# One order of all work replaced by another in a block-sparse attention kernel with a SoLU layer behind it

## The chip, the cores and the metric

The kernel runs on one core of a Trainium2 chip. The metric is device time in microseconds, the median of several executions; less is better. A core has five engines that run side by side, each through its own list of instructions in order: TensorE (PE: matrix multiplies, and transposes done as multiplies), VectorE (DVE), ScalarE (ACT), GpSimd (POOL) and SyncE (SP), which here only issues transfers. They wait for one another through semaphores. Transfers between the device memory and the core's memory (SBUF) are moved by 16 DMA engines.

## The reference

```python
# attention: batch 4, 8 heads, 768 positions, 64 wide; blocks of 32 positions
scores = scale * np.matmul(q, k.transpose(0, 1, 3, 2))
mask = np.abs(blk_i - blk_j) <= window          # neighbouring blocks
mask = mask | (blk_i == 0) | (blk_j == 0) | (blk_i == n_blocks - 1) | (blk_j == n_blocks - 1)
...                                             # and three sampled blocks for each block of queries
attn = softmax(np.where(mask, scores, -1000000000.0))
x = (attn @ v)                                  # brought to 3072 rows of 512
# the layer behind it: 512 -> 1024 -> 512
h = x @ w_in
solu = h * softmax(h)
ln = (solu - mu) / np.sqrt(var + 1e-06) * g_ln
out = ln @ w_out
```

## The kernel before

Nothing in the program is sorted out by a scheduler at run time. The kernel makes a list of some 1,130 operations (`op(...)`), each with the engine that runs it, the operations it depends on, the buffers it takes and the buffers whose last reader it is. A list of numbers, `ORDER` (lines 16 to 68), says in which order they are emitted. `Plan.run` walks through that list, checks that what an operation depends on came before it, and hands out buffers in the order in which they come free:

```python
        order = [self.ops[k] for k in ORDER]
        for o in order:
            assert all(d.done for d in o.deps + o.after)
            for p in o.take:
                o.slots[p] = self.pools[p].pop(0)
            for a, names in o.last_of:
                ...
                        self.pools[p].append(a.slots[p])
```

So `ORDER` sets two things: the order of the instructions on every engine, and which buffer each of them uses. An instruction whose input or buffer is late holds up everything behind it on its engine.

The operations, with the names used below (b is the batch, t one of three tiles of 256 queries, pr one of four pairs of heads, j one of 24 tiles of 128 output rows):

- Loads on SP (line 332): `load6/k1.0` brings the keys of batch 1, pair 0; there are three staging buffers each for k, q and v. Batch 0 is loaded in parts (`load2`, `load4`). The second weight matrix (`w_out`, line 377, two parts of 1 MB), the vector g (line 371) go through SP too; the first weight matrix (`w_in`, line 366) goes through POOL.
- Casts to bf16 on POOL: `cast6/q2.1` and so on (line 495 for k and q of batches 1 to 3, line 418 for v, lines 426 and 484 for batch 0). A cast gives the staging buffer free.
- Turning k and q so that the 64 columns of a head lie along the partitions: for batch 0 on TensorE with a copy by VectorE (`turn4`, `turn8`, lines 439 and 426); for batches 1 to 3 by a transposing transfer on SP (`cross_kq/k1.3`, line 497) and two copies by VectorE (`split/k1.3.0` and `.1`, line 501). A split overwrites the keys or queries of four pairs earlier, and waits for the last score that uses them. The mask of blocks is made at the start by POOL and VectorE, spread out by two small multiplies (`maskmm2`, `maskmm4`, line 305), and carried as 24 extra rows of k and q.
- Attention: for each (b, t, pr) three `score`s of 128x1024 on TensorE (line 523) into one of two score buffers, three exponentials on ScalarE (`exp`, line 528), one `pv` of 24 multiplies (line 542) into one of two accumulator banks (`mbank`), then `recip` and `norm` on VectorE (lines 551 and 554), which write x and give the bank free. There are eight buffers for the results of `exp`, and a `pv` frees three of them.
- The layer: x of 256 rows is turned by a transfer on SP (`cross_x`, line 585; on TensorE for the first and last tile, `turn2`, line 575). For each j two `feed4` (line 602) into one buffer of two banks, `silu_e` on ScalarE (line 624), `mult` on VectorE (line 627, which makes u and gives that buffer free), `stats` and `aggr` on VectorE (lines 634 and 637), `z2`, `vr` and `rs` on POOL (lines 640, 643 and 676). u is turned by a transfer on SP (`cross_u`, line 707). Two `out4` on TensorE (line 717) into an `mbank`, `scale` on VectorE (line 723, gives the bank free), `store` on SP (line 726). The last two tiles, 22 and 23, are done in halves (`half_e`, `half_m`, `half_s`, `feed3` and `feed1`, `outh`, `scaleh`).
- The weights `w_out` are multiplied with g and centred on VectorE (`wsum`, line 391; `wo`, line 405) between 20 and 54 us.
- `spare512`, `spare256`, `spare128`: multiplies of constants on TensorE that nobody reads (line 774), of 512, 256 or 128 columns. `SPARES` (line 15) lists their widths; they too have places in `ORDER`.

Of the kernel before, what the change touches and what calls it, by code (L numbers as in the profile page):

```python
# [11 lines left out]
ACT = mybir.ActivationFunctionType  # L12
PSUM = bass.MemoryType.PSUM

SPARES = (512, 512, 512, 512, 512, 512, 256, 256, 256, 256, 128, 128, 128, 128, 128, 128)
ORDER = [
# [52 lines left out]
]  # L69


# [15 lines left out]
class Plan:  # L87
# [9 lines left out]
    def op(self, name, eng, emit, deps=(), take=None, last_of=(), after=()):  # L97
        o = Op(name, eng, emit, deps, after, take, last_of)
        self.ops.append(o)
        return o  # L100
# [23 lines left out]
def kernel(  # L124
# [647 lines left out]

    for w in SPARES:
        s = op(f"spare{w}", "PE", lambda o, w=w: nc.tensor.matmul(
# [40 lines left out]
```

## Time and profile before

| | |
|---|---|
| time, median of 3 runs | 210.71 us (210.54 to 211.74) |
| profiled execution, its own time | 211.4 us |
| its span, first to last instruction | 209.7 us |
| granted TensorE clock in the record | 1.00 |
| busy: PE, DVE, ACT, POOL | 198.8, 147.6, 169.9, 72.1 us |
| instructions | 5757 |
| moved by DMA | 41.29 MB |

The profile shows one execution. A timeline row gives the start of an instruction or of a row of like ones, the time that it was busy, the engine, the line of the source, the operation, what it writes and reads, and in brackets how long the engine was idle before it and who ended that. "SPq" is SP's queue of transfer issues, where a row's time is the time to issue and not to land. Multiplies on TensorE overlap, so that the busy time of a row of them is longer than the distance to the next row; the distance between starts is what counts. An engine off the path that sets the end may be idle without cost.

### The profile page before, as it was taken

To read this page: it belongs to the slowest core of one execution; us is meant where nothing else is said; L and a number is where in the kernel's file an instruction comes from. 1 tells how busy PE (TensorE), PEld (TensorE's weight loads), DVE (VectorE), ACT (ScalarE), POOL (GpSimd) and SP (SyncE) were. 2 spreads that over 40 slices of the span, in tenths; PEclk is the share of its full clock that TensorE was granted. 3 is DMA by queue.
4 is the path that set the end of the run, shared out by engine and by line. 5 is a ranking of instruction groups with operands and counts; after the bars stand their busy time and mean duration, and the time that the engine had idled before them with its cause. 6 is when DMAs were issued, how large, how long until landed. Compare 5 with 4: busy or idle time off the path is not lost.

```text
span 209.7 us, 5757 instructions
## 1 busy us (share of the span) xinstructions
PE 198.8 (95%) x2257; PEld 140.0 (67%) x2289; DVE 147.6 (70%) x327; ACT 169.9 (81%) x210; POOL 72.1 (34%) x153
## 2 busy tenths in 40 slices
PE   7899999999979999989999999999999999999993
PEld 4698787666656676756656676766667677767452
DVE  5576579999997575896588626687876536449863
ACT  3399999997759879878788779998789989988470
POOL 7685322526057116424430811612120310010272
PEclk9999999999999999999999999999999999999999
DMA  5999998999999999989999997787842372542313
GB/s 137 301 360 343 322 164 296 181 315 301 222 316 265 307 188 260 280 181 282 194 323 204 234 196 175 99 174 95 188 100 53 92 111 69 87 100 53 101 62 143
DMA packets 71088, 41.29 MB, mean 197 GB/s; under 512 B 52236, under 2 KB 67092, under 8 KB 71060
## 3 DMA queue, kind: packets, MB, share of 16 engines
q1 hardware_dynamic: 69968, 39.86, 83.3%
q0 software_dynamic: 1056, 1.05, 3.0%
q8 instruction: 18, 0.29, 0.6%
q14 instruction: 10, 0.08, 0.1%
q10 hardware_dynamic: 36, 0.00, 0.0%
HBM read 23.07 MB, written 6.29 MB: 140 GB/s over the span
## 4 chain that ended last, share of the span: by engine, by line
PE 70%; DMA 8%; DVE 7%; ACT 5%; issue 4%; POOL 2%; SPq 2%; POOLq 0%; ACTq 0%
PE spairs L523 23%; PE mbank L717 15%; PE hpair L602 14%; PE mbank L542 13%; DMA uT<-u 5%; ACT ex L528 4%; PE hfirst L439 2%; DVE w_out_sb L405 2%; DMA qst<-in_q_dram 2%; PE sones L602 2%; DVE qT L501 2%; DMA kst<-in_k_dram 1%; DVE u L627 1%; SPq L332 1%; DVE kT L501 1%
## 5 line engine op out<-in xcount | busy, mean ns | idle before, releaser
L528 ACT ACTIVATE ex<-spairs 128x1024 bf16<-128x1024 f32 x144 | 140.6, 1025 | 25.4 <-PE spairs L523 24.1
L523 PE MATMUL spairs<-qT,kT 88*128 88x256 bf16 x576 | 82.3, 272 | 0.8 <-ACT ex L528 0.5
L523 PEld LDWEIGHTS <-kT 88*128 88x128 bf16 x576 | 53.1, 97 | 21.9 <-issue 3.0
L717 PE MATMUL mbank<-w_out_sb,uT 128*128 128x512 bf16 x172 | 45.5, 379 | 1.3 <-DMA uT<-u 0.3
L542 PEld LDWEIGHTS <-ex 128*128 128x128 bf16 x1152 | 41.5, 97 | 7.7 <-issue 3.0
L542 PE MATMUL mbank<-va,ex 128*128 128x65 bf16 x1152 | 42.9, 193 | 1.6 <-DVE x L554 0.8
L602 PE MATMUL hpair<-w_in_sb,xT 128*128 128x512 bf16 x156 | 42.8, 379 | 1.6 <-DMA xT<-x 0.4
L627 DVE TENSOR_TENSOR u<-hpair,e 128x1024 bf16<-128x1024 f32 x22 | 26.8, 1218 | 12.1 <-ACT e L624 11.8
L634 DVE BATCH_NORM_STATS2 bs<-u 128x6 f32<-128x512 bf16 x44 | 29.4, 680 | 0.3
L602 PEld LDWEIGHTS <-xT 128*128 128x128 bf16 x192 | 18.0, 97 | 14.8 <-DMA xT<-x 1.6
L717 PEld LDWEIGHTS <-uT 128*128 128x128 bf16 x184 | 17.0, 97 | 14.1 <-DMA uT<-u 1.3
L723 DVE TENSOR_SCALAR ot<-mbank,rs 128x512 f32<-128x512 f32 x23 | 17.2, 747 | 12.5 <-PE mbank L717 5.6
L643 POOL TENSOR_SCALAR vr<-z,mv 128x1 f32<-128x1 f32 x22 | 6.1, 276 | 55.0 <-DVE mv L637 52.4
L624 ACT ACTIVATE e<-hpair 128x1024 bf16<-128x1024 f32 x22 | 22.5, 1023 | 2.3 <-POOL vr L643 0.9
L551 DVE RECIPROCAL r<-mbank 128x4 f32<-128x4 f32 x48 | 8.3, 174 | 16.9 <-PE mbank L542 16.6
L554 DVE TENSOR_TENSOR x<-mbank,r 128x256 bf16<-128x256 f32 x48 | 19.6, 412 | 0.5
L495 POOL CAST qb<-qst 128x768 bf16<-128x768 f32 x12 | 10.7, 895 | 15.5 <-DMA qst<-in_q_dram 15.5
L418 POOL CAST va<-vst 128x768 bf16<-128x768 f32 x16 | 13.6, 853 | 6.7 <-DMA vst<-in_v_dram 6.6
L640 POOL TENSOR_TENSOR z<-z 128x1 f32<-128x1 f32 x22 | 4.2, 195 | 31.9 <-ACT e L624 30.6
L676 POOL TENSOR_TENSOR rs<-vr,neg_half 128x1 f32<-128x1 f32 x24 | 13.9, 581 | 1.2
L501 DVE COPY qT<-qx 64x768 bf16<-64x768 bf16 x24 | 11.8, 490 | 2.8 <-DMA qx<-qb 2.1
L495 POOL CAST kb<-kst 128x768 bf16<-128x768 f32 x12 | 10.1, 845 | 9.8 <-DMA kx<-kb 7.5
(90 smaller groups left out, 120.6 us busy)
## 6 DMA issues: line engine op xcount, KB each, us to landing
vst<-in_v_dram SPq DMA_DIRECT2D x16, 384.0 KB, 5.0
out_dram<-ot SPq DMA_DIRECT2D x23, 256.0 KB, 3.0
kst<-in_k_dram SPq DMA_DIRECT2D x15, 384.0 KB, 5.4
qst<-in_q_dram SPq DMA_DIRECT2D x12, 384.0 KB, 5.2
w_out_f<-in_moe_w_out_dram SPq DMA_DIRECT2D x2, 1024.0 KB
qst<-in_q_dram SPq DMA_DIRECT2D x4, 256.0 KB, 7.4
w_in_sb<-in_moe_w_in_dram POOLq DMA_DIRECT2D x2, 512.0 KB, 9.6
q0st<-in_q_dram SPq DMA_DIRECT2D x4, 128.0 KB, 2.9
```

What stands on the lines that cost most here:

```text
L495: ca = op(f"cast6/{nm}{b}.{pr}", "POOL", lambda o: nc.gpsimd.tensor_copy(out=cb[o.slot], in_=st[ld.slot].rearrange("p h c d -> p c h d")), ...
L501: got.append(op(f"split/{nm}{b}.{pr}.{hh}", "DVE", lambda o, hh=hh: nc.vector.tensor_copy(out=dst[0:D, sl, :, hh, :], in_=cx[t.slot][hh * ...
L523: nc.tensor.matmul(s[:, m, :], kT[0:KR, sl, jc, hh, :], qT[0:KR, sl, 2 * t : 2 * t + 2, hh, :], start=(m % 2 == 0), stop=(m % 2 == 1))
L528: exs.append(op(f"exp/{b}.{t}.{pr}.{n}", "ACT", lambda o, so=so: nc.scalar.activation(out=exb[o.slot], in_=banks("s", "pairs")[so.slot], f ...
L542: nc.tensor.matmul(acc(o)[:, qt, hh, :], exb[exs[n].slot][:, m, qt * P : (qt + 1) * P], va[i][:, 2 * pr + hh, jc, :], start=first, stop=(n ...
L554: nrm = op(f"norm/{b}.{t}.{pr}", "DVE", lambda o: nc.vector.tensor_tensor(out=xb[x_of[b, t].slot][:, :, 2 * pr * D : (2 * pr + 2) * D].rea ...
L602: nc.tensor.matmul(hb(n) if last else hb()[:, n, :], xTb[xt[0].slot][:, qt, c, :], w_in_sb[n][:, c, :], start=(c == 0), stop=(c == KD - 1))
L624: zs = op(f"silu_e/{j}", "ACT", lambda o: nc.scalar.activation(out=eb[o.slots["e"]], in_=hb().rearrange("p a f -> p (a f)"), func=ACT.Exp, ...
L627: us = op(f"mult/{j}", "DVE", lambda o: nc.vector.tensor_mul(out=ub[o.slot], in0=hb().rearrange("p a f -> p (a f)"), in1=eb[zs.slots["e"]] ...
L634: bs.append(op(f"stats/{j}.{n}", "DVE", lambda o, n=n: nc.vector.bn_stats(out=bsb[(bs[0] if bs else o).slot][:, n, :], in_=ub[us.slot][:, ...
L717: nc.tensor.matmul(mbank[m0.slot], uTb[ut[0].slot][:, KF // 2 * n + f, :], w_out_sb[n][:, f, :], start=(n == 0 and f == 0), stop=(n == 1 a ...
L723: fo = op(f"scale/{j}", "DVE", lambda o: nc.vector.tensor_scalar(out=otb[o.slot], in0=mbank[os_[0].slot], scalar1=rsb[rs.slot], scalar2=No ...
```

## The change

`ORDER` is another list, and `SPARES` has 19 entries for 16: 4,096 columns in all for 4,864. Everything else is the same text; the operations and their dependencies are the same.

```diff
-SPARES = (512, 512, 512, 512, 512, 512, 256, 256, 256, 256, 128, 128, 128, 128, 128, 128)
+SPARES = (512, 512, 512, 256, 256, 256, 256, 128, 128, 128, 128, 128, 128, 128, 128, 128, 128, 128, 128)
 ORDER = [
-    0, 9, 21, 31, 1115, 3, 7, 1126, 32, 1123, 1121, 1114, 4, 33, 22, 13, 1119, 12, 2, 14, 1116, 24, 35, 11, 15,
...
+    1124, 0, 21, 31, 1115, 2, 115, 11, 32, 1114, 3, 4, 5, 13, 33, 12, 14, 22, 15, 86, 9, 6, 16, 35, 23, 17, 18,
...
```

Written out by name, engine by engine, the two orders run close together. These are the places that the prediction speaks of. The start, on each engine:

```
PE   before  11 spares (3,584 columns) turn4/k0.0 maskmm2 spare512 spare256 turn4/q0.0 turn8/k0.2 spare256 score/0.0.0.0
             turn4/q1.0 score/0.0.0.1 turn4/k1.0 turn8/k1.2 score/0.0.0.2
     after   spare128 spare512 spare512 maskmm2 turn4/k0.0 spare256 spare128 spare512 spare128 turn4/q0.0 turn8/k0.2 spare128
             turn4/q1.0 score/0.0.0.0 score/0.0.0.1 spare128 turn8/k1.2 turn4/k1.0 score/0.0.0.2
POOL before  ... ident sel2 sel2 cast4/k0.0.2 cast2/q0.1.0 maskc2 cast6/k0.1.0 sel4 cast6/k0.2.0
     after   ... ident maskc2 ones cast4/k0.0.2 sel4 cast2/q0.1.0 sel4 cast6/k0.1.0 vones cast6/k0.2.0
SP   before  k0.0 q0.0 k0.0 q0.1 k0.1 k0.2 q0.2 q0.3 v0.0 k0.3 q0.0 q0.1 g v0.1 v0.2 w_out q0.2 v0.3 k1.0 q0.3 w_out
     after   k0.0 q0.0 k0.0 g q0.1 k0.1 k0.2 k0.3 v0.0 q0.2 q0.3 v0.1 q0.0 w_out q0.1 q0.2 v0.2 v0.3 k1.0 q0.3 w_out
```

From 45 to 65 us:

```
POOL before  z2/1 q1.2 k1.3 vr/0 v1.0 q1.3 rs/0 q2.1 v1.2 v1.1 vr/1 rs/1 q2.0          (k, q, v: casts)
     after   z2/2 k1.3 q1.3 vr/0 z2/1 v1.1 rs/0 v1.2 vr/1 rs/1 v1.3 q2.0 k2.0 vr/2 rs/2 v2.0 k2.2 z2/3 vr/3 v2.1 rs/3 q2.1
SP   before  ... cross_kq/q1.2 cross_kq/q1.3 v1.2 cross_kq/k1.3 q2.1 cross_x/0.2 k2.1 store/0 q2.2 q2.3 cross_u/2 v1.3
     after   ... cross_kq/k1.2 cross_u/2 cross_kq/q1.3 cross_kq/k1.3 k2.0 cross_x/0.2 v1.2 store/0 q2.1 v1.3 q2.2 v2.0 store/1 cross_u/3
PE   before  pv/1.0.0 out4/1.0 score/1.0.2.0 out4/1.1 score/1.0.2.1 score/1.0.2.2 feed4/4.0 pv/1.0.1 score/1.0.3.0 score/1.0.3.1
             feed4/4.1 score/1.0.3.2 pv/1.0.2 out4/2.0
     after   pv/1.0.0 score/1.0.2.0 score/1.0.2.1 pv/1.0.1 out4/1.0 score/1.0.2.2 score/1.0.3.0 out4/1.1 feed4/4.0 score/1.0.3.1
             feed4/4.1 score/1.0.3.2 pv/1.0.2 score/1.1.0.0 out4/2.0
DVE  before  split/q1.3.1 stats/1.0 mult/3 norm/1.0.0 split/k1.3.0 split/q1.3.0 split/k1.3.1
     after   norm/1.0.0 split/k1.3.1 split/q1.3.1 recip/1.0.1 split/q1.3.0 split/k1.3.0 mult/3 stats/1.0
```

From 85 to 92 us, and the end:

```
DVE  before  recip/1.2.0 stats/7.0 split/q2.1.1 split/k2.0.1 norm/1.2.0 scale/5
     after   split/q2.1.0 recip/1.2.0 aggr/6 split/q2.1.1 mult/7 scale/5 norm/1.2.0
PE   before  pv/1.2.0 out4/5.0 score/1.2.1.2 score/1.2.2.0 out4/5.1 score/1.2.2.1 pv/1.2.1
     after   pv/1.2.0 score/1.2.1.2 out4/5.0 score/1.2.2.0 out4/5.1 score/1.2.2.1 feed4/8.0 score/1.2.2.2 pv/1.2.1
DVE  before  half_m/22.0 aggr/21 half_m/22.1 half_m/23.0 uevac4/22.0 scale/20 half_m/23.1 scale/21 uevac4/23.0
     after   half_m/22.0 scale/19 half_m/23.0 half_m/22.1 uevac4/22.0 aggr/21 half_m/23.1 scale/20 uevac4/23.0 scale/21
```

102 rows, old and new, of the table ORDER are left out of this document.

## The prediction

> **What bounds the kernel now.** I read the page's busy times first, then the stages, then the chain that ended last, and last the queues at the places where that chain leaves TensorE. The page's first row and a table of stages (columns: stage, its length, busy us and instruction count of TensorE, its weight loads, VectorE, ScalarE and POOL, then granted clock, DMA share and GB/s):
>
> ```profile
> PE 198.8 (95%) x2257; PEld 140.0 (67%) x2289; DVE 147.6 (70%) x327; ACT 169.9 (81%) x210; POOL 72.1 (34%) x153
> 0.00:10.00 10.00, 7.95 (x59) 5.32 (x60) 5.10 (x18) 4.03 (x5) 6.52 (x21) 1.00 0.73 213
> ...
> 36.00:57.00 21.00, 19.74 (x211) 13.44 (x212) 20.27 (x41) 17.83 (x25) 7.68 (x11) 1.00 1.15 256
> 57.00:68.00 11.00, 9.43 (x99) 6.30 (x99) 9.45 (x18) 8.24 (x10) 6.93 (x12) 1.00 1.24 296
> ...
> 88.00:110.00 22.00, 21.06 (x226) 14.00 (x227) 16.59 (x36) 17.32 (x21) 9.50 (x16) 1.00 1.16 242
> 110.00:206.60 96.60, 95.35 (x1030) 64.94 (x1044) 63.26 (x144) 80.20 (x106) 23.39 (x59) 1.00 0.62 123
> ```
>
> From 110 us to the last matmul TensorE is idle for 96.60 - 95.35 = 1.25 us: nothing but fewer columns would shorten that part, and the orders hold the same columns there. An order can win in front of it: 2.05 us idle in the first 10, 1.26 in 36 to 57 (where VectorE, 20.27 of 21.00, is the bound), 1.57 in 57 to 68, 0.94 in 88 to 110. The chain of waits shows what the third of these is:
>
> ```profile
> 54.20 3.81 DMA qst<-in_q_dram
> ...
> 58.06 0.83 POOL qb L495
> ...
> 58.91 0.37 SPq L332
> ...
> 59.33 5.53 DMA uT<-u
> ...
> 64.90 0.39 PE mbank L717
> ...
> 65.94 0.88 PE spairs L523 x8
> 66.81 0.87 PE mbank L717 x4
> 67.68 0.47 PE spairs L523 x4
> 68.14 0.73 PE mbank L542 x24
> ```
>
> Read from the bottom: out4/2.0 waits for the transposed u of row tile 2, whose transfer was issued at 59.33, because SP stood behind a load of q (58.91) that wanted a buffer, which POOL gave free with a cast (58.06) that waited for another load (54.20). The last four rows give what dense work costs: two scores 0.88, half an output or feed 0.87, one score 0.45, one pv 0.73. Against these, TensorE's own timeline (start, busy, idle before and who ended it):
>
> ```profile
> 57.50 1.07 PE L523 MATMUL spairs<-qT,kT 88*128 88x256 bf16 x8
> 58.99 1.04 PE L602 MATMUL hpair<-w_in_sb,xT 128*128 128x512 bf16 x3 [0.43 <-DMA xT<-x]
> 60.74 0.89 PE L542 MATMUL mbank<-va,ex 128*128 128x65 bf16 x24 [0.71 <-POOL va L418]
> ...
> 63.67 0.90 PE L542 MATMUL mbank<-va,ex 128*128 128x65 bf16 x24
> 64.90 1.04 PE L717 MATMUL mbank<-w_out_sb,uT 128*128 128x512 bf16 x3 [0.33 <-DMA uT<-u]
> ```
>
> Scores at 57.50 need 0.88, feed4/4.0 starts at 58.99: 0.61 lost to the transposed x. That feed needs 0.87, pv/1.0.1 starts at 60.74: 0.88 lost to the cast of v. pv/1.0.2 needs 0.73, the output starts at 64.90: 0.50 lost. Together 2.0 us, more than the idle column says, since a matmul's modelled end hides 0.2 to 0.3 of each gap.
>
> **The change, part by part.** Instructions on VectorE, ScalarE, POOL and SP are the same ones in another order. TensorE has 19 filler matmuls of 4,096 columns for 16 of 4,864.
>
> *POOL and SP at 50 to 65 us.* The rows of POOL, then SP, then VectorE:
>
> ```profile
> 58.06 0.82 POOL L495 CAST qb<-qst 128x768 bf16<-128x768 f32 x1 [7.32 <-DMA qst<-in_q_dram]
> 58.83 1.86 POOL L418 CAST va<-vst 128x768 bf16<-128x768 f32 x2
> ...
> 54.89 1.24 SPq L585 DMA_TRANSPOSE xT<-x  x1
> ...
> 46.66 1.21 DVE L627 TENSOR_TENSOR u<-hpair,e 128x1024 bf16<-128x1024 f32 x1
> ...
> 53.38 0.42 DVE L554 TENSOR_TENSOR x<-mbank,r 128x256 bf16<-128x256 f32 x1
> ```
>
> POOL stood 7.32 us in cast6/q2.1, with the casts of v1.2 and v1.1 behind it; u of tile 2 was ready at 46.66 + 1.21 = 47.9 and its transfer left at 59.33. After the change cast6/v1.1 stands directly behind vr/0, cast6/q2.1 stands fifteen instructions behind it, and cross_u/2 stands on SP ahead of cross_kq/q1.3, far in front of those loads of q: it leaves at about 49. So the waits of 0.88 and 0.50 have lost what made them. The 0.61 stays: cross_x/0.2 needs norm/0.2.3, which ran at 53.38 and has 0.35 us (one split) more VectorE work ahead of it, and this stage is VectorE's. With the 0.6 of the opening (below) the transfer leaves at 54.9 to 55.2 and feed4/4.0 can start at about 59.2, against 58.99. But TensorE has by then also done pv/1.0.1 and one score more, 0.73 + 0.45 = 1.18 us of work that it had ahead of it before. Sum up to pv/1.0.3: -1.18 - 0.88 - 0.50 + 0.2 = -2.36; I keep +0.3 for short waits of VectorE for the splits of k1.3, which now stand ahead of mult/3, and take -2.1. That includes the opening. Bounds: +0.5 (all three waits return elsewhere and the opening is paid) and -2.9 (opening free).
>
> *88 to 110 us.* VectorE's rows and TensorE's pv/1.2.1:
>
> ```profile
> 88.69 0.95 DVE L501 COPY qT<-qx 64x768 bf16<-64x768 bf16 x1 [0.37 <-PE spairs L523]
> 89.56 0.97 DVE L501 COPY kT<-kx 64x768 bf16<-64x768 bf16 x1
> 90.56 0.42 DVE L554 TENSOR_TENSOR x<-mbank,r 128x256 bf16<-128x256 f32 x1
> ...
> 89.82 0.60 PE L523 MATMUL spairs<-qT,kT 88*128 88x256 bf16 x4
> 91.04 0.89 PE L542 MATMUL mbank<-va,ex 128*128 128x65 bf16 x24 [0.62 <-DVE x L554]
> ```
>
> There are two accumulator banks; pv/1.2.1 waits for norm/1.2.0 to empty one, and that stood behind two splits. The score at 89.82 needs 0.45, so 91.04 - 90.27 = 0.77 us are lost. In the new order the splits of q2.1, mult/7 and scale/5 stand before norm/1.2.0, about 3.1 us after score/1.2.1.2, but TensorE has out4/5.0, a score, out4/5.1, a score, feed4/8.0 and a score before pv/1.2.1: 3 x 0.87 + 3 x 0.45 = 3.96 us. The bank is free in time. The stage's other idle time is 0.94 - 0.62 = 0.32; I take -0.8 for the stage, between 0 (other splits take their place) and -1.1.
>
> *The opening.* TensorE, then ScalarE, POOL, SP:
>
> ```profile
> 0.83 3.15 PE L774 MATMUL mbank<-const-bfloat16-1.0 128*128 128x512 bf16 x11 [0.83 <-PEq L799]
> 3.77 0.63 PE L439 MATMUL hfirst<-ident,kc 128*88 128x128 bf16 x4
> 4.63 0.20 PE L305 MATMUL mbank<-allow_b,selp 24*128 24x24 bf16 x2 [0.23 <-DVE allow_b L287]
> ...
> 9.03 0.87 PE L439 MATMUL hfirst<-ident,kc 128*88 128x128 bf16 x12 [0.99 <-POOL kc L426]
> ...
> 10.37 13.76 ACT L528 ACTIVATE ex<-spairs 128x1024 bf16<-128x1024 f32 x14 [1.19 <-PE spairs L523]
> ...
> 8.14 0.83 POOL L426 CAST kc<-kst 128x768 bf16<-128x768 f32 x1 [2.02 <-DMA kst<-in_k_dram]
> ...
> 8.40 0.41 SPq L371 DMA_DIRECT2D g_row<-in_moe_g_ln_dram  x1
> ```
>
> From 10.37 on ScalarE runs its exponentials end to end; what starts that run is the third one, and it hangs on the load of k0.1, cast at 8.14. Now three fillers of 1,152 columns stand ahead of the mask's matmul and then TensorE waits for allow_b; the table of g is issued ahead of k0.1 on SP, 0.41 us and its gap; POOL waits for the mask (copy to qc, memset of onesf) before it casts the rest of k0.0, and turn4/q1.0 stands ahead of the first score, so the first exponential is about a microsecond later. That is before the point that counts: k0.1's cast moves from 8.14 to at most 8.6. Besides, the eleven fillers took 2.94 us for 3,584 columns, 0.82 ns a column, and the twelve transposes at 9.03 took 0.70 for 1,536, 0.46 ns: TensorE starts at about half pace, though the granted clock reads 1.00 in the stage's row. With its dense work beginning near 4.5 instead of 0.83 the slow pace should last longer. Between that cast and the third exponential lie twelve transposes and a score, 12 x 128 + 4 x 256 = 2,560 columns, 2,560 x 0.36 ns = 0.92 us more if all are slow; I count half of that, and 0.1 to 0.2 for the load: +0.6 for the start of the run; bounds 0.1 (only the load) and 2.5 (slow for four more exponentials). The load of w_out is moved ahead of q of pairs 1 and 2 and v0.2, v0.3; by the bytes ahead of them these land at 18 to 23 us, each just ahead of its use, so I cost that at nothing; a late v0.2 would hold back the exponentials one for one.
>
> [...]
>
> *The end.* half_m/23.1 stands ahead of scale/20 now, but TensorE works up to 206.6 either way: -0.1. For 110 us on, where the margins are other ones, I add +0.3 (0 to +1.0).
>
> Sum against the profiled execution's own 211.4 (span 209.7 and 1.7 around it): -2.1 - 0.8 - 0.1 + 0.3 = -2.7, so 208.7. That execution is 0.7 over the median of 210.71; in terms of the median, **208.0**.
>
> **The rivals.** [...]
> (B) The waits only change place: TensorE, held up by VectorE's splits of k1.3 or by its wo products, has not done the 1.18 us before feed4/4.0, and the late 0.8 returns: 208.0 + 1.2 + 0.8 = 210.0. For it: VectorE is full from 36 to 57.
> (C) Slower: the load of v1.2, before at 51.38, now stands on SP behind cross_x/0.2 and leaves at about 56.1. This row is the loads of v:
>
> ```profile
> DMA to landing us min/median/max: 3.7/5.0/9.5
> ```
>
> With 5.0 its cast ends at 61.95, just as TensorE asks for pv/1.0.2; behind it on POOL stand vr/1, rs/1 and the cast of v1.3, behind those scale/1 and store/1. With 9.5 it ends at 66.45 against pv/1.0.2 at 63.67 before: 2.8 later, less the 0.50, less the late 0.8 or not: 210.7 + 2.8 - 0.5 + 0.3 - 0.1 = 213.2, or 212.4 with the late gain; I take 213.0, since v1.3 follows on the same queue. It decides against the change from a landing of 7.7 on.
>
> **How the numbers follow.** Forecast 0.52, A 0.14, B 0.18, C 0.16. One per cent (about what a measurement of this kernel can tell from no change) is 208.6 and 212.8. The forecast's own range is 206.4 to 209.2; 0.46 of its 0.52 lie below 208.6, 0.06 above. A and B lie within. C lies above, and I count into its 0.16 the like of it at other loads. Faster 0.46, same 0.06 + 0.14 + 0.18 = 0.38, slower 0.16. The range runs from all gains at their bounds (-2.9 - 1.1 - 0.1 = -4.1, with a little kept back: 206.2) to just short of C: 212.6.
>
> **What would show it.** Right: POOL's idle time of 7 us before a cast of q is gone, cross_u/2 leaves SP near 49, TensorE reaches pv/1.0.3 near 66 instead of 67.98, no idle time over 0.4 at 88 to 110, and the end of the last matmul some 2.7 earlier. The opening: third exponential at 10.5 to 11.2. Wrong: a wait of TensorE for v over 0.5 us near 62, slow matmuls after 10 us, or a TensorE idle time of over 2 us after 110.

## The result, and the profile after

The changed kernel takes 207.97 us, the median of 6 executions (207.44 to 208.95), against 211.23 (210.34 to 212.09, 6) for the kernel before: a ratio of 0.990, 95% interval 0.9864 to 0.9936. In a later set of runs it came to 207.59 (207.04 to 208.71, 12), ratio 0.9899 (0.9865 to 0.9932). Medians in this document are over all executions; the ratios and their intervals leave out executions more than 1.5% above the fastest of the same kernel in the same set, and so a ratio is not always the quotient of two medians.

The profiled execution of the changed kernel took 207.91 with a span of 206.2 (before 211.4 and 209.7). Its busy times and the same table of stages as in the prediction (TensorE, its weight loads, VectorE, ScalarE, POOL, granted clock, DMA share, GB/s):

```profile
PE 198.3 (96%) x2292; PEld 141.3 (69%) x2292; DVE 146.8 (71%) x327; ACT 170.5 (83%) x210; POOL 73.0 (35%) x153
0.00:10.00 10.00, 6.65 (x49) 5.02 (x50) 4.98 (x16) 3.28 (x5) 7.34 (x24) 1.00 0.71 214
...
36.00:57.00 21.00, 20.52 (x246) 14.59 (x244) 19.96 (x42) 19.32 (x25) 8.46 (x12) 1.00 1.13 215
57.00:68.00 11.00, 11.00 (x131) 7.62 (x128) 9.72 (x21) 9.38 (x12) 4.01 (x6) 1.00 1.02 299
68.00:88.00 20.00, 20.00 (x227) 13.85 (x226) 14.37 (x32) 17.28 (x22) 10.82 (x22) 1.00 1.14 244
88.00:110.00 22.00, 22.00 (x257) 15.22 (x256) 16.11 (x36) 18.98 (x23) 6.34 (x12) 1.00 1.21 269
110.00:203.10 93.10, 92.70 (x1008) 62.96 (x1006) 62.53 (x141) 78.07 (x102) 24.11 (x59) 1.00 0.60 131
```

TensorE's idle time, stage by stage: 3.35 us in the first ten (before 2.05), 0.48 for 1.26 from 36 to 57, 0.00 for 1.57 from 57 to 68, 0.00 for 0.94 from 88 to 110, and 0.40 for 1.25 behind 110. The opening is dearer than before, every stage from 36 us on is cheaper, and from 57 to 110 us TensorE never stops. The place where the chain of waits stood before, on TensorE, POOL, SP and VectorE:

```profile
58.45 1.04 PE L523 MATMUL spairs<-qT,kT 88*128 88x256 bf16 x8
59.32 1.03 PE L717 MATMUL mbank<-w_out_sb,uT 128*128 128x512 bf16 x4
60.19 1.03 PE L602 MATMUL hpair<-w_in_sb,xT 128*128 128x512 bf16 x4
...
66.57 0.89 PE L542 MATMUL mbank<-va,ex 128*128 128x65 bf16 x24
...
60.94 0.82 POOL L418 CAST va<-vst 128x768 bf16<-128x768 f32 x1 [6.31 <-DMA vst<-in_v_dram]
...
49.39 1.26 SPq L707 DMA_TRANSPOSE uT<-u  x1
...
55.17 1.23 SPq L585 DMA_TRANSPOSE xT<-x  x1
56.45 0.77 SPq L332 DMA_DIRECT2D vst<-in_v_dram  x1
...
52.01 1.40 DVE L405 SCALAR_TENSOR_TENSOR w_out_sb<-w_out_f,g_sb,wbar 128x512 bf16<-128x512 f32 x2
```

No row of TensorE there has a bracket: nothing is waited for. POOL still stands 6.31 us, but in a cast that is early enough. pv/1.0.3 starts at 66.57 instead of 67.98.

To add up waits that the modelled ends hide, I take the distance between the starts of successive operations on TensorE, less what each takes in dense work (0.45 for a score, 0.73 for a pv, 0.87 for half a feed or output, 0.22 to 0.45 for turns, 0.053 for 128 columns of filler, my estimate, where the traces of before and of the changed kernel show 0.054 to 0.060 at the fast pace), and call it the loss. The slow pace of the opening counts as loss too. The table gives it up to and with the operation named, then from there on; a small negative number is the rounding of those durations, and differences of 0.3 or less can be such rounding. "New" and "old" say which order a kernel (below) has in that stretch.

| kernel | to score/0.2.0.2 (34 us) | to pv/1.0.3 (67) | to score/2.0.2.2 (107) | to the end |
|---|---|---|---|---|
| before | old 5.91 | old 3.99 | old 1.32 | old 0.33 |
| changed | new 7.61 | new 1.20 | new -0.27 | new -0.45 |
| changed, again | new 7.35 | new 0.93 | new -0.26 | new -0.49 |
| h1, first run | old 6.66 | new 0.96 | new 0.76 | new -0.48 |
| h1, second run | old 6.37 | new 0.65 | new 0.77 | new -0.39 |
| h2 | new 8.39 | old 3.47 | old 0.69 | old 0.06 |
| c1 | old 5.85 | old 4.61 | new 0.41 | new -0.58 |
| c2 | old 5.82 | old 3.41 | old 1.03 | new -0.52 |
| b1, b2, b3 | 6.15, 5.37, 6.56 | 2.52, 4.41, 2.69 | 1.84, 0.43, 1.28 | -0.06, -0.05, -0.30 |

### The profile page after: what moved, and what is told of

Same layout as the page of the kernel before. It is cut to its first block, busy times and chain, and to the rows that moved or that the text cites. A ratio compares the mean times of both kernels' runs of the same rounds, so it can differ in the third digit from the quotient of the medians.

```text
span 206.2 us, 5792 instructions
## 1 busy us (share of the span) xinstructions
PE 198.3 (96%) x2292; PEld 141.3 (69%) x2292; DVE 146.8 (71%) x327; ACT 170.5 (83%) x210; POOL 73.0 (35%) x153
## 4 chain that ended last, share of the span: by engine, by line
PE 67%; DMA 15%; POOL 7%; issue 4%; DVE 4%; SPq 1%; ACT 0%; POOLq 0%; DVEq 0%; ACTq 0%
PE spairs L523 22%; PE mbank L717 16%; PE hpair L602 15%; PE mbank L542 12%; DMA qst<-in_q_dram 5%; DMA kst<-in_k_dram 4%; DMA vst<-in_v_dram 3%; DMA kx<-kb 3%; POOL kb L495 1%; PE sones L602 1%; SPq L497 1%; POOL va L418 1%; DVE u L654 1%; POOL rs L676 1%; DVE ot L723 1%
## 5 line engine op out<-in xcount | busy, mean ns | idle before, releaser
L523 PE MATMUL spairs<-qT,kT 88*128 88x256 bf16 x576 | 84.4, 274 | 0.9 <-ACT ex L528 0.6
L717 PE MATMUL mbank<-w_out_sb,uT 128*128 128x512 bf16 x184 | 47.1, 379 | 0.0
L602 PE MATMUL hpair<-w_in_sb,xT 128*128 128x512 bf16 x176 | 45.0, 379 | 0.0
L723 DVE TENSOR_SCALAR ot<-mbank,rs 128x512 f32<-128x512 f32 x23 | 17.2, 747 | 11.2 <-POOL rs L676 6.9
L418 POOL CAST va<-vst 128x768 bf16<-128x768 f32 x16 | 14.6, 910 | 14.1 <-DMA vst<-in_v_dram 13.9
L495 POOL CAST qb<-qst 128x768 bf16<-128x768 f32 x12 | 10.2, 856 | 7.5 <-DMA qst<-in_q_dram 6.0
L501 DVE COPY kT<-kx 64x768 bf16<-64x768 bf16 x24 | 9.2, 383 | 2.2 <-DMA kx<-kb 1.8
```

Source lines behind the costliest of these rows:

```text
L418: ready_v[(b, pr)] = op(f"cast6/v{b}.{pr}", "POOL", lambda o: nc.gpsimd.tensor_copy(out=va[i][:, 2 * pr : 2 * pr + 2, :, 0:D], in_=vst[ld. ...
L495: ca = op(f"cast6/{nm}{b}.{pr}", "POOL", lambda o: nc.gpsimd.tensor_copy(out=cb[o.slot], in_=st[ld.slot].rearrange("p h c d -> p c h d")), ...
L523: nc.tensor.matmul(s[:, m, :], kT[0:KR, sl, jc, hh, :], qT[0:KR, sl, 2 * t : 2 * t + 2, hh, :], start=(m % 2 == 0), stop=(m % 2 == 1))
L602: nc.tensor.matmul(hb(n) if last else hb()[:, n, :], xTb[xt[0].slot][:, qt, c, :], w_in_sb[n][:, c, :], start=(c == 0), stop=(c == KD - 1))
L717: nc.tensor.matmul(mbank[m0.slot], uTb[ut[0].slot][:, KF // 2 * n + f, :], w_out_sb[n][:, f, :], start=(n == 0 and f == 0), stop=(n == 1 a ...
L723: fo = op(f"scale/{j}", "DVE", lambda o: nc.vector.tensor_scalar(out=otb[o.slot], in0=mbank[os_[0].slot], scalar1=rsb[rs.slot], scalar2=No ...
```

## The experiments

**The start and the rest apart.** h1 has the order of before up to score/0.1.0.2 (which TensorE starts at 21 to 23 us) and the changed order behind it; h2 the other way round. The fillers go with the parts: h1 has 5,632 columns of them and h2 3,328. Before, on the same chip: 211.10 (209.15 to 212.07).

```diff
-ORDER = the changed order
+ORDER = h1: before up to score/0.1.0.2, then what is left, in the changed order
+ORDER = h2: changed order up to score/0.1.0.2, then what is left, in the order of before
```

> The old order up to score/0.1.0.2 (about 21 us), the new order behind it. Theory (the two stretches are worth what they are worth by themselves: the new start costs 1.4 us, all later changes give 4.7): about 206.5, 1.4 under the new order; the exponentials run from 10.4 and silu_e/0 starts near 35.0. Rival (the two halves of an order only fit together): new waits at the seam, 208 or more.

> The new order up to score/0.1.0.2, the old one behind it. Theory: the start alone costs 1.4 us, so about 212.6 against 211.2 for the old order. Rival (the gain is spread over the whole order, the start costs nothing at the end): 211 or less.

Measured: h1 206.54 (205.97 to 208.37), ratio 0.9807 (0.973 to 0.9884); h2 211.55 (210.44 to 211.90), ratio 1.0021 (0.9949 to 1.0092). The gain comes with the new rest and not with the new start. What the new start costs with the old rest behind it, h2 can't tell: its interval runs from 1.1 us below before to 1.9 above, and the expected 1.4 lies in it, as does nothing at all. Its trace loses 8.39 up to 34 us.

**What the new start costs.** ScalarE's exponentials in the changed kernel, and the first exponential of the layer (`silu_e/0`, line 624) as the mark; the last row is the same mark before:

```profile
8.81 6.00 ACT L528 ACTIVATE ex<-spairs 128x1024 bf16<-128x1024 f32 x6 [4.22 <-PE spairs L523]
15.07 2.85 ACT L528 ACTIVATE ex<-spairs 128x1024 bf16<-128x1024 f32 x3 [0.25 <-PE spairs L523]
...
18.52 1.94 ACT L528 ACTIVATE ex<-spairs 128x1024 bf16<-128x1024 f32 x2 [0.60 <-PE spairs L523]
20.35 0.19 ACT L256 ACTIVATE warm<-const-float32-0.0 1x1 f32<-1x1 f32 x1
...
36.39 1.03 ACT L624 ACTIVATE e<-hpair 128x1024 bf16<-128x1024 f32 x1
...
35.02 1.04 ACT L624 ACTIVATE e<-hpair 128x1024 bf16<-128x1024 f32 x1
```

The third exponential starts at 8.81 + 2 x 1.00 = 10.81, 0.44 later than before's 10.37; two gaps of 0.25 and 0.60 follow, and 0.09 for the small activation that the new order puts between exponentials: 1.38 in all, and the mark is 1.37 later. The cast of k0.1, which the prediction had at up to 8.6, began at 8.09 (before 8.14), so the 0.44 is not the load's. Three kernels try to take parts of the loss away. In a1 the loads of q0.2 and q0.3 come first again:

```diff
 SP    (loads)
-k0.2 k0.3 v0.0 q0.2 q0.3 v0.1
+k0.2 q0.2 k0.3 q0.3 v0.0 v0.1
 POOL  (casts)
-cast6/v0.1 ... cast2/q0.3.0
+cast2/q0.3.0 cast6/v0.1
```

> The new order, but on SP the loads of q0.2 and q0.3 go ahead of k0.3 and v0.0 as in the old one, and on POOL the cast of q0.3 goes ahead of the cast of v0.1. Theory (most of what the start lost went at the sixth to tenth exponential, where the queries of pairs 2 and 3 were late: gaps of 0.25 and 0.60): about 0.85 faster than the new order, 207.1, both gaps gone, third exponential still near 10.8. Rival (slow pace of TensorE made the loss): no change, 208.0.

Measured: 208.34 (207.47 to 209.01), ratio 0.9875 (0.9803 to 0.9947). The loads alone are not it: the gaps stay, at 0.34 and 0.60.

```profile
15.28 2.85 ACT L528 ACTIVATE ex<-spairs 128x1024 bf16<-128x1024 f32 x3 [0.34 <-PE spairs L523]
18.73 1.94 ACT L528 ACTIVATE ex<-spairs 128x1024 bf16<-128x1024 f32 x2 [0.60 <-PE spairs L523]
```

They end with scores, and what stands ahead of those scores on TensorE is its own order of turns: turn4/q2.0 behind score/0.0.1.2, and turn4/q3.0, turng, turn8/q0.2, a filler and turn2 between score/0.0.2.2 and score/0.0.3.0. In a2 the early fillers are back, 2,432 columns ahead of the mask's multiply, to have TensorE at its fast pace earlier:

```diff
 PE
-spare128 spare512 spare512 maskmm2
+spare128 spare512 spare512 spare512 spare512 spare512 spare512 spare256 spare128 maskmm2
```

> The new order with 2,432 more columns of fillers ahead of the mask's first multiply, 3,584 as in the old one. Rival of a1 (slow pace): the fast pace comes near 6 us instead of near 9.4, the third exponential moves from 10.8 to about 10.4, and 0.4 us or more of the loss goes: 207.5. Theory of a1 (loads): the gaps of 0.25 and 0.60 stay; if only the load of k0.1 gates the third exponential, no change at all.

Measured: 208.06 (207.98 to 208.29), ratio 0.9866 (0.98 to 0.9932), no different from the changed kernel's 0.990. Its first scores and exponentials:

```profile
7.22 1.04 PE L523 MATMUL spairs<-qT,kT 88*128 88x256 bf16 x8
...
7.86 5.82 ACT L528 ACTIVATE ex<-spairs 128x1024 bf16<-128x1024 f32 x6 [3.74 <-PE spairs L523]
14.82 2.86 ACT L528 ACTIVATE ex<-spairs 128x1024 bf16<-128x1024 f32 x3 [1.13 <-PE spairs L523]
...
12.22 0.40 POOL L426 CAST qc<-q0st 128x256 bf16<-128x256 f32 x1 [2.92 <-DMA q0st<-in_q_dram]
```

The scores are fast and the exponentials begin 0.95 earlier, and then wait 1.13 instead of 0.25 for the seventh score. In front of that score on TensorE stand turn4/q2.0 and pv/0.0.0. The last row is the cast that the first of them waited for, and the cast of v for the second stands behind it: with the slow pace gone, the load of q0.2 came too late. a1 has that load early (its cast began at 9.58) and keeps the slow pace; no kernel here has both, so that the two together cost nothing is not shown. a3 is a1 with the turns moved ahead of the scores, and VectorE's copies with them:

```diff
 PE    (beside the edit of a1)
-score/0.0.1.2 ... turn4/q2.0     turn8/k3.2 ... turn4/k3.0     score/0.0.2.2 ... turn4/q3.0
+turn4/q2.0 score/0.0.1.2         turn4/k3.0 turn8/k3.2         turn4/q3.0 score/0.0.2.2
```

> The new order with the loads and casts of a1 and, on TensorE, turn4/q2.0 ahead of score/0.0.1.2, turn4/k3.0 ahead of turn8/k3.2 and turn4/q3.0 ahead of score/0.0.2.2 (with VectorE's copies), as in the old order. Theory (the gaps of 0.25 and 0.60 come from turns that stand between a score and the next, with no buffer free to work ahead): both gaps of ScalarE go, 0.8 us faster than the new order, about 207.2. Rival (other work then fills the same time, or the data are late there anyway): gaps move on, 208.

Measured: 208.35 (207.32 to 209.05), 0.9948 (0.9924 to 0.9972) of before on its chip (median there 209.77), so it is no faster than the changed kernel was against before. The 0.60 is gone, and its place is taken by more and smaller gaps:

```profile
10.91 3.10 ACT L528 ACTIVATE ex<-spairs 128x1024 bf16<-128x1024 f32 x3 [0.16 <-PE spairs L523]
14.29 1.02 ACT L528 ACTIVATE ex<-spairs 128x1024 bf16<-128x1024 f32 x1 [0.28 <-PE spairs L523]
15.70 3.05 ACT L528 ACTIVATE ex<-spairs 128x1024 bf16<-128x1024 f32 x3 [0.38 <-PE spairs L523]
18.93 1.94 ACT L528 ACTIVATE ex<-spairs 128x1024 bf16<-128x1024 f32 x2 [0.18 <-PE spairs L523]
```

In a3 turn4/q2.0 waits 0.32 us for a copy by VectorE, and the score behind it comes that much later. So the order of turns made the 0.60; what made the 0.25 stays open.

**The two moves that I had held for the gain, alone.** Made in the order of before: b1 moves the transposed u up on SP, b2 the casts of v up on POOL, b3 both. Before, on the same chip: 209.77 (208.0 to 214.1).

```diff
 SP    (b1, b3)
-cross_x/0.2 k2.1 store/0 q2.2 q2.3 cross_u/2 v1.3
+cross_x/0.2 cross_u/2 k2.1 store/0 q2.2 q2.3 v1.3
 POOL  (b2, b3)
-rs/0 q2.1 v1.2 v1.1 vr/1
+rs/0 v1.1 v1.2 q2.1 vr/1
```

> The old order with one move on SP: cross_u/2 directly behind cross_x/0.2 instead of behind the loads of k2.1, q2.2 and q2.3. Theory (two separate stalls behind cast6/q2.1): u of tile 2 lands near 61, out4/2.0 no longer waits, 0.5 us faster; TensorE's waits for x (0.6) and v1.1 (0.9) stay. Rival (the stage is held by VectorE and nothing there is gained): no change.

> The old order with one move on POOL: the casts of v1.1 and v1.2 ahead of cast6/q2.1. Theory: pv/1.0.1 no longer waits (0.9 us), but the transposed u of tile 2 lands at 64.9 as before, so TensorE arrives at out4/2.0 earlier and waits there 0.9 longer: no change in the time. Rival (each stall has its own price): 0.9 faster.

> The old order with both moves. Theory: 0.88 + 0.50 = 1.4 us faster than the old order, and TensorE reaches pv/1.0.3 near 66.6 instead of 67.98; all that the new order does elsewhere at 36 to 68 us is worth the rest of its 2.8 there. Rival (one move is worth nothing without VectorE's and TensorE's new order): under 0.5.

Measured: b1 210.88, ratio 1.0079 (1.0043 to 1.0115); b2 209.76, ratio 1.0024 (0.9987 to 1.006); b3 210.88, ratio 1.006 (1.0028 to 1.0092). b2 did as expected: its time is that of before, the wait of pv/1.0.1 is gone (0.87 lost before, 0.01 now), and out4/2.0 lost 1.29 instead of 0.50. Both of the expected gains, of b1 and of b3, failed, and their medians lie 1.1 us above before's. TensorE's waits of b3:

```profile
67.34 0.89 PE L542 MATMUL mbank<-va,ex 128*128 128x65 bf16 x24 [0.85 <-POOL va L418]
...
75.91 1.04 PE L602 MATMUL hpair<-w_in_sb,xT 128*128 128x512 bf16 x4 [0.56 <-DMA xT<-x]
...
105.42 1.02 PE L602 MATMUL hpair<-w_in_sb,xT 128*128 128x512 bf16 x4 [0.58 <-DVE u L627]
```

The waits that before had at 58.99, 60.74 and 64.90 are gone from it, as meant. Two others have come in their place, for the next tile of v and for the next x; what POOL did ahead of the first:

```profile
66.46 0.83 POOL L418 CAST va<-vst 128x768 bf16<-128x768 f32 x1 [2.38 <-DMA vst<-in_v_dram]
```

Neither input is much later than before. v1.3 landed at 66.41 (before 66.04) and the transposed x at 75.86 (75.25): TensorE gets there sooner and finds that the next load has not come. The third wait, for a u at 105.42, is not the moves' doing: it is there too, with 0.68 and 0.69, in c2 and h2, which have the order of before unchanged at that place (last section). Rival B of the prediction, that the waits only change place, is what the small edit does. The changed kernel has moved v1.3 ahead of q2.2 and cross_x/1.0 ahead of cross_kq/q2.1 as well, and shows none of the three. Why b1 and b3 came out slower than before, and not the same, I can't place: their traces are 1.0 and 1.25 shorter than the one profiled execution of before, which comes from an earlier set of runs.

**A ladder.** c2 takes the changed order from score/2.0.2.2 (107 to 109 us), c1 from score/1.0.3.2 (62 to 64 us), h1 from score/0.1.0.2 (21 to 23 us; two of the expectations call it 24); beside them, on one chip, the changed kernel itself. Before there: 210.22 (208.23 to 214.85).

```diff
-ORDER = order of before
+ORDER = c2: before up to score/2.0.2.2, then what is left, in the changed order
+ORDER = c1: before up to score/1.0.3.2, then what is left, in the changed order
```

> The order of before up to score/2.0.2.2 (the cut lies at about 109 us), the changed order behind it. Theory 'the gains of the stages add': the traces of before and of the changed kernel show only 0.4 to 0.5 us less lost by TensorE behind 110 us, so 0.4 us less than before, about 0.998. Rival 'a stage's gain is only kept if the next stages are the new ones, and most of it is made by what the new late order allows': 1 us or more below before, under 0.995.

> The order of before up to score/1.0.3.2 (about 62 us), the changed order behind it. So the transposed u of tile 2 still leaves SP at 59 us and the waits for it, for x and for v stay; the late norm/1.2.0 and everything behind is as in the changed kernel. Theory 'the gains add': 0.4 from behind 110 us and 1.9 from 68 to 110 us, so 2.3 us below before, about 0.989. Rival 'given back': the old queue of loads reaches into the new part, and the time is within 0.5 us of before, 0.998 or more.

> The kernel with the start of before (up to score/0.1.0.2, about 24 us) and the changed order behind it, once more, on one chip with the changed kernel itself. Theory 'the new start costs 1.4 us and nothing behind it gives that back': 1.2 to 1.6 us below the changed kernel of this call, about 0.981 of before. Rival 'the first time was chance': within 0.5 us of the changed kernel.

> The changed kernel itself, beside the three others on one chip: 0.987 of before, as at first (0.9846). It is the foot of the ladder: before, new from 112 us, new from 62 us, new from 24 us, all new.

| changed order from | median, us | ratio to before |
|---|---|---|
| never | 210.22 | |
| 108 us (c2) | 210.36 (208.75 to 214.94) | 1.0026 (0.9987 to 1.0065) |
| 63 us (c1) | 209.58 (208.04 to 210.47) | 0.9999 (0.9967 to 1.0031) |
| 22 us (h1) | 207.04 (206.24 to 208.62) | 0.9890 (0.9832 to 0.9947) |
| 0 us (the changed kernel) | 207.59 (207.04 to 208.71) | 0.9899 (0.9865 to 0.9932) |

Most of the gain comes with the order between 22 and 63 us, where the new order follows behind it: from c1 to the changed kernel the median falls by 2.0 us, from c1 to h1 by 2.5. That the new order behind 63 us gives 2.3 us by itself, as I expected of c1, is wrong: c1's median lies 0.6 us below before's, its ratio is 0.9999, and its interval ends 0.7 us below before. Between h1 and the changed kernel lie 0.55 us of medians, less than the 1.2 to 1.6 expected, with overlapping intervals: that leaving the old start costs anything is not shown by the times. The traces say where the old start's lead goes: the mark `silu_e/0`, expected near 35.0, stands at 36.16 and 35.79 in h1's two traces, against 36.39 and 36.14 in those of the changed kernel, since ScalarE waits 0.49 and 0.61 near 26 us, behind the seam. h1 had the lowest median on both chips (206.54, 207.04). TensorE's waits between 49 and 62 us in c1, which has the order of before there:

```profile
50.00 0.61 PE L699 MATMUL mbank<-ident,u 128*128 128x128 bf16 x8 [0.49 <-DVE x L554]
52.06 0.89 PE L542 MATMUL mbank<-va,ex 128*128 128x65 bf16 x24 [0.59 <-DVE uT L703]
56.49 1.02 PE L717 MATMUL mbank<-w_out_sb,uT 128*128 128x512 bf16 x4 [0.47 <-DVE ot L723]
60.10 1.04 PE L602 MATMUL hpair<-w_in_sb,xT 128*128 128x512 bf16 x4 [0.38 <-DMA xT<-x]
61.83 0.89 PE L542 MATMUL mbank<-va,ex 128*128 128x65 bf16 x24 [0.69 <-POOL va L418]
```

Neither profiled execution of the changed kernel has a bracket on TensorE between 44 and 64 us. The waits for x and v (0.38 and 0.69) are those of the prediction's rows at 58.99 and 60.74. The wait for v is the kernel's: in all five traces with the order of before there and that cast not moved (before, c1, c2, h2, b1) it lost 0.81 to 0.87. The wait for x lost 0.22 to 0.57 in the same five. The three ahead of them, all for VectorE, are 0.47 to 0.59 here and were 0.21 or too short for a bracket in the prediction's execution, in the same order of instructions. The wait for u at 64.90, 0.33 in the prediction's execution, was 0.29 in h2 and absent in c2, which have it in the same order (the 1.13 of b2 is the wait that its edit pushed there). The 0.62 at 91.04 was 0.35 in b1 and absent in b2, b3, c2 and h2. So some of the waits of one trace are that execution's alone.

What remains open: whether the order from 22 to 63 us keeps its gain without the new one behind it, and which of its moves make it. b3 lost what its two moves saved, but no kernel had the old start, the new middle and the old rest.

## Why the prediction was right or wrong

The forecast of 208.0 stands against 207.97, and 208.7 for the profiled execution against 207.91. Against the times of the ladder the sum stands well: from c1 to the changed kernel, which is the opening and the middle, the median falls by 2.0 (forecast 2.1), and the order behind 63 us gives 0 to 0.6 (forecast 0.6). In the traces the terms did not all come out: the opening cost about 1 us more than its term and the late stages gave about 2 us more than theirs. And what the terms were put down to holds only in part. By the table of losses:

- *The opening, +0.6 (0.1 to 2.5).* Measured +1.70 in the first pair of traces (7.61 for 5.91), +1.44 in the second of the changed kernel (7.35), and +1.37 at ScalarE's mark. Within the bounds, and mis-sized in the trace: the third exponential did start at 10.81 as forecast (10.5 to 11.2), but the step took this start as all that counts, and two gaps of ScalarE came behind it. Neither the loads alone (a1) nor the pace alone (a2) takes them away; the order of turns made the longer one (a3). In time the cost is smaller than in the trace: 0.55, not told from nothing.
- *36 to 68 us, -2.1 with the opening in it, so -2.7 by itself.* Measured 1.20 for 3.99: -2.8, and -3.1 in the second trace; other traces with the old order there lost 3.41 to 4.61. The three waits were read rightly, but a modelled end hides 0.17 to 0.18 of each and not 0.2 to 0.3. cross_u/2 left SP at 49.39 (forecast 49), cross_x/0.2 at 55.17 (54.9 to 55.2), and the waits of 0.88 and 0.50 are gone. That the 0.61 for x would stay was wrong: TensorE, with pv/1.0.1 and one more score done, reaches feed4/4.0 only at 60.19, when x is there (landed at 59.34). And the reason given for the term does not carry it: the same two moves alone gain nothing (b1, b2, b3), so that its size came out by luck as far as it was put down to them. What the rest of the new order does there is not taken apart.
- *88 to 110 us, -0.8 (0 to -1.1).* In the traces the stretch from 68 to 109 us gave -1.6. In time c1 gives 0.0 by its ratio, with at most 0.7 for everything behind 63 us. The step that failed is the reading of a wait of 0.77 in one execution as the kernel's: with the same order, b2, b3, c2 and h2 do not have it.
- *Behind 110 us, +0.3, and the end, -0.1.* In the traces -0.8; in time nothing (c2).
- *The median 0.7 below the profiled execution.* The changed kernel's profiled execution lies at its median (207.91 and 207.97), so part of the late gain that the two traces show can be just that difference of executions of before.
- *The range.* The sum of all gains at their bounds gives 210.7 - 4.1 = 206.6; the 206.2 of the prediction lies 0.4 below it, with nothing "kept back".
- *Rival A*, a slow pace of TensorE that lasts, did not happen. TensorE stayed slow up to 9.4 us, in its timeline of the changed kernel:

```profile
7.72 1.88 PE L523 MATMUL spairs<-qT,kT 88*128 88x256 bf16 x8
9.42 0.23 PE L774 MATMUL mbank<-const-bfloat16-1.0 128*128 128x128 bf16 x1
9.50 0.83 PE L439 MATMUL hfirst<-ident,kc 128*88 128x128 bf16 x12
10.16 0.60 PE L523 MATMUL spairs<-qT,kT 88*128 88x256 bf16 x4
```

  Two scores, 2,048 columns, took 1.70, 0.83 ns each; twelve transposes, 1,536 columns, took 0.66, 0.43 ns each. The fast pace came 5.0 us after the dense work had begun at 4.47, with a granted clock of 1.00 in the stage's row. Before, with dense work from 0.83 on, it came at 6.1 to 6.2. h2 has the opening of the changed kernel, and there the same two scores took only 0.91, from 7.71 on; in a2 they took 0.88, from 7.22 on, and a2 was not faster. So with the same opening the fast pace came 1.7 us earlier in one execution than in the other, and what brings it is not shown. The opening's upper bound of 2.5, an estimate, has the slow pace last for four more exponentials; in the changed kernel it was over ahead of the third, at 10.81, and the opening lost 1.37 to 1.70 in all.
- *Rival B* did not happen to the change, but happens to its two visible moves when they are made alone.
- *Rival C* came close: the load of v1.2 left at 56.45 (forecast 56.1), its cast ended at 61.76 (61.95), and TensorE asked for it at 62.79. 1.0 us later it would have been a wait.

## What to carry to other kernels

A wait of a trace is one draw. Before a term of a forecast is built on it, look whether a second execution, or a kernel with the same order at that place, has it too; the wait for v near 60 us came back each time, and the one at 91 us in two of six traces. A wait that comes back is not yet worth its length: with the one for v taken away (b2), TensorE waited about as much longer for the next input. Where several inputs are late in a row, moving one of them up brings the engine sooner to the next, and the gain came here only with an order that moved many of them. Where two kernels differ by a whole order, cutting the orders at several points and joining them tells in a few runs which stretch carries the difference.

## What the runs showed of the hardware that was not expected

A VectorE split (64x768 bf16, line 501) takes 0.35 us, or up to 1.04. In the fourteen traces of this case, 68 of 672 took over 0.6 (9 of 48 before, 3 of 48 after), and each of the 68 ran beside a cast on POOL. VectorE's splits and POOL's casts before, near 59 us:

```profile
58.36 0.73 DVE L501 COPY kT<-kx 64x768 bf16<-64x768 bf16 x1
59.02 0.98 DVE L501 COPY qT<-qx 64x768 bf16<-64x768 bf16 x1
60.03 0.86 DVE L501 COPY kT<-kx 64x768 bf16<-64x768 bf16 x1
```

The casts ran from 58.06 to 60.69 (58.83 + 1.86), two of them in that last row of 1.86. The first split ended at 59.09, 0.21 after the cast of q; the last at 60.89, 0.20 after the last cast by these rounded rows. So it is for all 68: each ends 0.21 to 0.22 after a cast. The other way round, a cast of the changed kernel:

```profile
52.04 2.06 POOL L418 CAST va<-vst 128x768 bf16<-128x768 f32 x1 [1.79 <-DMA vst<-in_v_dram]
```

It took 2.06 for 0.82, having started 0.03 after VectorE began its multiplies of w_out (the row at 52.01 in the first section), and it ended at 54.10, 0.69 after these. So in these rows the slowed instruction of the one engine ended only behind that of the other, by 0.20 to 0.69. Why, no run here shows.

In this kernel it has a price. The groups of splits, before and after (busy us, mean ns):

```profile
L501 DVE COPY qT<-qx 64x768 bf16<-64x768 bf16 x24 | 11.8, 490 | 2.8 <-DMA qx<-qb 2.1 <-PE spairs L523 0.4
L501 DVE COPY kT<-kx 64x768 bf16<-64x768 bf16 x24 | 9.9, 418 | 2.8 <-PE spairs L523 1.7 <-DMA kx<-kb 0.9
...
L501 DVE COPY kT<-kx 64x768 bf16<-64x768 bf16 x24 | 9.2, 383 | 2.2 <-DMA kx<-kb 1.8
L501 DVE COPY qT<-qx 64x768 bf16<-64x768 bf16 x24 | 9.0, 375 | 1.1 <-PE spairs L523 0.7
```

21.7 us before, 18.2 after (18.6 in the second trace): 3.5 us of VectorE. Between 36 and 64 us, where VectorE is busiest, the splits of before took 2.9 us more than 0.35 each, those of c1 2.2, of c2 2.8, of b2 2.2, of h2 1.7, of b1 1.7, of b3 0.6; in both runs of the changed kernel and of h1 it is 0.0, in a2 0.5. That goes along with the gain and is likely part of it, but no experiment here took the overlap away by itself, and b3, with 0.6, was not faster. Where it is seen to become a wait of TensorE is a split ahead of a `mult`, and there the same order shows both cases. Before, then c2, in the order of before near 104 us:

```profile
104.12 0.35 DVE L501 COPY qT<-qx 64x768 bf16<-64x768 bf16 x1
...
106.09 1.04 PE L602 MATMUL hpair<-w_in_sb,xT 128*128 128x512 bf16 x4
...
102.66 0.92 DVE L501 COPY qT<-qx 64x768 bf16<-64x768 bf16 x1
...
104.77 1.02 PE L602 MATMUL hpair<-w_in_sb,xT 128*128 128x512 bf16 x4 [0.68 <-DVE u L627]
```

Of the six traces with this order there, the split took 0.35 in two (before, b2) and 0.92 to 1.04 in four (b1, b3, c2, h2); TensorE waited for that u in those four, 0.58 to 0.69, and in neither of the two. In the two, the cast on POOL began 0.41 and 0.06 us after the split; in the four, between 0.11 before it and 0.01 after. So a tenth of a microsecond decides, and this is one way in which executions of one order come to differ. h1 lost 0.77 in both of its traces behind such a split, here in the second:

```profile
92.76 0.94 DVE L501 COPY qT<-qx 64x768 bf16<-64x768 bf16 x1
...
95.01 1.02 PE L602 MATMUL hpair<-w_in_sb,xT 128*128 128x512 bf16 x4 [0.77 <-DVE u L627]
```

In the changed kernel this split took 0.36, and feed4 there waits for nothing. The prediction had two such splits in its rows, 0.95 and 0.97 at 88.69 and 89.56, and took them for the normal price.

Executions of one kernel differ more than its instructions suggest: the median of before ran from 209.8 to 211.2 over four sets of runs. A change of 1% is safely told only beside runs of the same set.
